# Both PSUM banks of the fourth convolution group: matmuls first, then casts

## The chip, the cores and the metric

The kernel runs on one core of one Trainium2 chip. The metric is the device time of one execution in microseconds (us). The time before is the median of 6 runs: 434.73 us, lowest 433.61, highest 435.31. The engines are written as in the profile: PE is TensorE (PEld its weight loads), ACT is ScalarE, DVE is VectorE, POOL is GpSimd, SP is SyncE. L342 is line 342 of the kernel before.

## What is computed

A light convolution over time (8 heads of 24 channels, 7 taps, causal, softmaxed taps) is followed by an RWKV channel mix. Shapes: x is 8 x 4160 x 192, the hidden width is 1024.

```python
# attn: w = softmax(weight); y[b,s,c] = sum_k w[head(c),k] * x_pad[b,s+k,c]
x_prev = np.concatenate([np.zeros((B, 1, D)), x[:, :-1, :]], axis=1)   # x is y from above
xk = mu_k * x + (1.0 - mu_k) * x_prev
xr = mu_r * x + (1.0 - mu_r) * x_prev
k = np.maximum(xk @ w_k, 0.0)
v = k * k @ w_v
r = 1.0 / (1.0 + np.exp(-(xr @ w_r)))
return (r * v).astype(np.float32)
```

## The kernel before

**The work.** The 8 sequences are taken as 4 pairs. A pair's 4160 rows are cut into steps of up to 512 rows (the first pair begins with a step of 256, and the last rows of all pairs make the last step). For each step DVE forms `d` (L472), `xk` and `xr` (L495, L499) from the transposed convolution `yT`; PE multiplies `xk` by `w_k` into `ps_k` tiles (L519); ACT takes the ReLU to `k_sb` (L548); DVE squares it to `k` (L562); PE multiplies `xr` by `w_r` (L593) and ACT takes the sigmoid (L601); PE multiplies `k` by `w_v` into `ps_v` (L576); DVE multiplies by the sigmoid into `o_sb` (L617); SP stores it.

**The order.** It is written out by hand, per engine, in bundles. A bundle has four slots, each one `ps_k` tile of 6 matmuls. Within a bundle the calls come in this order: loads due (`early`), the four K tiles and their ReLUs, `r`, transposes due (`first`), `v`, the mixes, three squares, `v_out`, the convolutions due (`xt`), the fourth square, then `late`. Each engine keeps this order for its own instructions.

**PSUM.** Every matmul result goes to one pool, `ring`: four buffers of two banks each. A new tile takes a buffer that an older tile has left, and its first matmul waits until the reader of the older tile is done.

**The convolution.** It is done in groups of blocks. The first pair's first four groups (3, 4, 4 and 5 blocks of 120 rows) are cast to `y` and transposed on PE (`tr`, L419, copied by DVE at L428 into `yT`). All later groups use 64-row pieces (`conv_mm` at L321, `conv_out` at L384), are written to DRAM (`y_write`, L400) and read back transposed (`y_read`, L406).

The change is in `conv_full`, which is called for the fourth group alone (g = 3, 5 blocks, rows 1320 to 1919 of the first pair), twice (c = 0 and c = 1), both in bundle 1. One call covers four heads. It takes one `ring` tile, two heads in each of its two banks; a bank gets two matmuls (L342, 240 columns each), and then its 48 columns per block are cast by ACT to `y` (L351). Columns are cut at multiples of 64, so that a bank takes one cast (120x480) or two (120x160 and 120x320): c = 0 has one and then two, c = 1 has two and then one. Six casts in all.

Around it, in bundle 1: the K tiles k4 to k7, `r`, the transposes of the third group (g = 2), then the two `conv_full` calls; then bundle 2: K tiles k8 to k11, `r`, the transposes of g = 3 (two tiles: four blocks, one block), `v`, two units of the fifth group's convolution; then k12 and on. The ring buffers go round accordingly: the two convolution tiles take the buffers of k6 and k7, k8 and k9 those of `r` and the transposes, k10 and k11 those of the two convolution tiles; the next `r`, the two transpose tiles and `v` take those of k8 to k11.

Of the kernel before, what the change touches and what calls it, by code (L numbers as in the profile page):

```python
# [14 lines left out]
def kernel(  # L15
# [60 lines left out]
    n = 0  # L76
# [109 lines left out]
    n = groups[0][2] * 2 * D  # L186
# [113 lines left out]
    def pieces(c0, c1):  # L300
        cuts = [c0] + [a for a in range(Q, D, Q) if c0 < a < c1] + [c1]
        return list(zip(cuts, cuts[1:]))
# [28 lines left out]
    def conv_full(g, c, copy):  # L331
        nb = groups[g][2]
        if c == 0:
            ys[g] = two.tile([P, GB, 2 * D], BF16, tag="y", name="y")
        y = ys[g][:BLK, :nb, :].rearrange("p n (c s q) -> p n c s q", c=NC, s=2)
        ps2 = ring.tile([P, 2, BANK], FP32, tag="k", name="ps_c")
        w = 2 * G
        for k in range(2):
            ps = ps2[:, k, 0 : nb * 2 * w].rearrange("p (n s c) -> p n s c", n=nb, s=2)
            for i in range(2):  # L340
                h = 4 * c + 2 * k + i
                nc.tensor.matmul(  # L342
                    out=ps[:, :, :, i * G : (i + 1) * G],
                    lhsT=toe[:, h, :],
                    rhs=xbs[g][:, :nb, :, h * G : (h + 1) * G],
                    start=True,
                    stop=True,
                )
            c0 = (4 * c + 2 * k) * G
            for a, b in pieces(c0, c0 + w):  # L350
                copy(  # L351
                    out=y[:, :, a // Q, :, a % Q : a % Q + b - a], in_=ps[:BLK, :, :, a - c0 : b - c0]
                )
# [300 lines left out]
    def conv(g, c):  # L654
        if g < 3:
            act_, dve_ = nc.scalar.copy, nc.vector.tensor_copy
            return conv_small(g, (act_, act_, dve_ if g == 0 else act_))
        if g == 3:
            return conv_full(g, c, nc.scalar.copy)
        conv_mm(g, c)  # L660
        conv_out(g, c, nc.scalar.copy)
# [153 lines left out]
```

## Time and profile before

| | |
|---|---|
| median of 6 runs | 434.73 us |
| profiled execution | 434.74 us |
| its span, first to last instruction | 433.0 us |
| mean granted TensorE clock | 0.996 |
| busy: PE, DVE, ACT, POOL | 97%, 87%, 80%, 14% of the span |
| HBM traffic over the span | 156 GB/s |
| L342, matmuls of `conv_full` | 8 of 262 to 268 ns, 23.4 to 26.5 us |
| L351, casts of `conv_full` | 6 of 292 to 700 ns, 24.1 to 26.8 us |

The profiled execution lies at the median. Some 1.7 us of its time lie outside the span. PE, DVE and ACT are all well filled, and so the averages say little about one place: the change touches 3 us near the start, and what it meets there is read from the timeline of those microseconds, engine by engine. In a timeline row the columns are start, duration of the row (neighbouring instructions of one kind are merged), engine, line, operation, output and input, count, and in brackets the idle time before it with what ended it.

### The profile page before, as it was taken

Reading aid. Unit: us, or ns where it says so; the run is one execution under the profiler, and the core shown is the slowest. Engines: PE = TensorE matmul, PEld = TensorE weight load, DVE = VectorE, ACT = ScalarE, POOL = GpSimd, SP = SyncE. Lnnn points to the kernel's source line nnn. Section 1 sums busy time; section 2 is a strip of 40 time slices with the busy share of each in tenths; the row PEclk is TensorE's granted clock in tenths of the full one; section 3 lists DMA queues with packets and bytes.
Section 4 is the critical chain, followed back from the end, with each engine's and each line's share of the span. In section 5 each row is a group of like instructions: output and inputs, shape, how many; then the busy total and the mean of one; then the engine's idle time right before and its main releaser. Section 6 shows DMA issues by size and latency. Waiting matters only on the chain.

```text
span 433.0 us, 12070 instructions
## 1 busy us (share of the span) xinstructions
PE 419.4 (97%) x5045; PEld 293.5 (68%) x5045; DVE 377.2 (87%) x678; ACT 348.0 (80%) x427; POOL 62.4 (14%) x101
## 2 busy tenths in 40 slices
PE   7779999999999999999999999999999999999995
PEld 3447677667867766776677667766766776667785
DVE  5859978888988899888889989888898889999983
ACT  5786988888988888888889878988898888777780
POOL 7661002113300200303030200203000000000000
PEclk9989999999999999999999999999999999999999
DMA  7998694999796976679796994496846484321223
GB/s 130 192 159 125 170 188 105 197 218 205 175 186 177 177 195 124 97 189 169 181 185 161 184 205 108 97 224 131 182 122 132 117 204 88 111 66 47 74 75 109
DMA packets 136444, 64.73 MB, mean 149 GB/s; under 512 B 87122, under 2 KB 136006, under 8 KB 136390
## 3 DMA queue, kind: packets, MB, share of 16 engines
q1 hardware_dynamic: 96536, 48.29, 46.7%
q0 software_dynamic: 38960, 15.08, 29.9%
q8 instruction: 39, 0.64, 0.6%
q10 hardware_dynamic: 894, 0.61, 0.5%
q14 instruction: 15, 0.12, 0.1%
HBM read 30.75 MB, written 36.96 MB: 156 GB/s over the span
## 4 chain that ended last, share of the span: by engine, by line
PE 90%; ACT 3%; DVE 3%; DMA 2%; issue 1%; POOL 1%; DVEq 0%; ACTq 0%
PE ps_v L576 40%; PE ps_k L519 38%; PE ps_r L593 7%; PE ps_c L321 4%; ACT k_sb L548 2%; DMA wk<-in_moe_w_k_dram 2%; DVE k L562 1%; DVE o_sb L617 0%; POOL xb L155 0%; ACT y L351 0%; PE ps_t L419 0%; ACT y L384 0%; DVE yT L428 0%; DVE xk L499 0%; DVE xk L495 0%
## 5 line engine op out<-in xcount | busy, mean ns | idle before, releaser
L548 ACT ACTIVATE k_sb<-ps_k 128x1024 bf16<-128x1024 f32 x260 | 246.3, 1046 | 23.1 <-PE ps_k L519 22.7
L519 PE MATMUL ps_k<-xk,wk 64*128 64x512 bf16 (+1 forms) x1632 | 182.2, 370 | 2.9 <-ACT k_sb L548 1.2
L576 PE MATMUL ps_v<-wv,k 128*128 128x192 bf16 x2080 | 182.7, 246 | 0.5 <-ACT k_sb L548 0.5
L576 PEld LDWEIGHTS <-k 128*128 128x128 bf16 x2080 | 168.6, 98 | 10.5 <-issue 10.4
L562 DVE TENSOR_TENSOR k<-k_sb 128x1024 bf16<-128x1024 bf16 x260 | 167.2, 684 | 0.4 <-ACT k_sb L548 0.4
L519 PEld LDWEIGHTS <-wk 64*128 64x128 bf16 x1632 | 75.1, 94 | 89.8 <-issue 11.7
L617 DVE TENSOR_TENSOR o_sb<-ps_v,r_sb 128x768 f32<-128x768 f32 x64 | 61.2, 956 | 35.4 <-PE ps_v L576 31.6
L384 ACT CAST y<-ps_c 128x960 bf16<-128x960 f32 (+7 forms) x81 | 50.7, 667 | 45.4 <-PE ps_c L321 45.4
L134 POOL DMA_DIRECT2D xb<-in_x_dram x56 | 40.3, 732 | 205.5 <-PE ps_k L519 158.8
L601 ACT ACTIVATE r_sb<-ps_r 128x768 bf16<-128x768 f32 x65 | 56.0, 862 | 1.3 <-PE ps_r L593 1.3
L593 PEld LDWEIGHTS <-xr 64*128 64x128 bf16 x780 | 34.1, 94 | 16.2 <-DVE xb L112 1.3
L593 PE MATMUL ps_r<-wr,xr 64*128 64x192 bf16 x780 | 42.9, 243 | 0.9 <-DVE xb L112 0.8
L499 DVE TENSOR_TENSOR xr<-xr,yT 128x1536 bf16<-128x1536 bf16 (+1 forms) x33 | 31.0, 939 | 1.1
L472 DVE TENSOR_TENSOR d<-yT 128x1536 bf16<-128x1536 bf16 (+2 forms) x35 | 31.1, 888 | 0.7 <-DMA yT<-y_dram 0.6
L499 DVE TENSOR_TENSOR xk<-xk,yT 128x1536 bf16<-128x1536 bf16 (+1 forms) x32 | 30.4, 950 | 1.1
L495 DVE TENSOR_SCALAR xk<-d,mu 128x512 bf16<-128x512 bf16 (+1 forms) x99 | 30.3, 361 | 1.2
L495 DVE TENSOR_SCALAR xr<-d,mu 128x512 bf16<-128x512 bf16 (+1 forms) x102 | 29.3, 343 | 0.0
L321 PE MATMUL ps_c<-xb,toe 64*64 64x240 bf16 (+1 forms) x448 | 20.0, 265 | 0.0
L321 PEld LDWEIGHTS <-toe 64*64 64x64 bf16 x448 | 8.3, 105 | 7.7 <-issue 7.7
L456 POOL COPY y_tail<-yT 128x195 bf16<-128x195 bf16 x4 | 1.5, 383 | 69.6 <-DMA yT<-y_dram 69.6
L428 DVE COPY yT<-ps_t 128x720 bf16<-128x720 bf16 (+1 forms) x7 | 3.2, 500 | 6.5 <-PE ps_t L419 6.5
L131 POOL DMA_DIRECT2D xb<-in_x_dram x14 | 7.6, 544 | 1.4 <-POOL xb L114 0.9
(55 smaller groups left out, 58.5 us busy)
## 6 DMA issues: line engine op xcount, KB each, us to landing
out_dram<-o_sb SPq DMA_DIRECT2D x128, 192.0 KB
xb<-in_x_dram POOLq DMA_DIRECT2D x36, 240.0 KB, 6.5
y_dram<-y SPq DMA_DIRECT2D x22, 360.0 KB
xb<-in_x_dram POOLq DMA_DIRECT2D x10, 216.0 KB, 5.2
y_dram<-y SPq DMA_DIRECT2D x22, 75.0 KB
y_dram<-y SPq DMA_DIRECT2D x6, 216.0 KB
xb<-in_x_dram POOLq DMA_DIRECT2D x6, 144.0 KB, 5.9
xb<-in_x_dram POOLq DMA_DIRECT2D x4, 192.0 KB, 7.6
```

What stands on the lines that cost most here:

```text
L134: nc.gpsimd.dma_start(out=xb[i * Q : (i + 1) * Q, full[0] : full[-1] + 1, s, :], in_=bass.AP(tensor=x.tensor, offset=x.offset + (b * S + b ...
L321: nc.tensor.matmul(out=ps[j * Q : (j + 1) * Q, i, 0 : nb * w].rearrange("p (n s c) -> p n s c", n=nn, s=2)[:, :, :, k * G : (k + 1) * G], ...
L384: copy(out=y[:, :, :, a // Q, :, a % Q : a % Q + b - a], in_=src[:, :, :, :, a - c0 : b - c0])
L495: nc.vector.tensor_scalar(out=t[:, c, :L], in0=d[:, c, :L], scalar1=mu[:, i, c : c + 1], scalar2=None, op0=ALU.mult)
L499: nc.vector.tensor_tensor(out=o, in0=o, in1=y_of(s, sl, 0), op=ALU.add)
L519: nc.tensor.matmul(out=ps[:, i, f * L : (f + 1) * L], lhsT=wk[r, c, fs], rhs=xk[r, c, :L], start=c == 0 and f == 0, stop=c == NC - 1 and f ...
L548: nc.scalar.activation(out=k_sb, in_=ps.rearrange("p a b -> p (a b)"), func=AF.Relu)
L562: nc.vector.tensor_tensor(out=o, in0=i, in1=i, op=ALU.mult)
L576: nc.tensor.matmul(out=o, lhsT=k2s[s][:, f, t * P : (t + 1) * P], rhs=wv[:, f, :], start=(f == 0), stop=(f == NF - 1),)
L593: nc.tensor.matmul(out=ps[:, i, k * D : (k + 1) * D], lhsT=xr[q, c, ts], rhs=wr[q, c, :], start=c == 0, stop=c == NC - 1,)
L601: nc.scalar.activation(out=r_sbs[s, j], in_=ps[:, :, 0 : 2 * D], func=AF.Sigmoid)
L617: nc.vector.tensor_tensor(out=o_sb.rearrange("p (b t) d -> p b (t d)", b=2), in0=v_ps.pop((s, j)), in1=r_sbs.pop((s, j)), op=ALU.mult,)
```

## The change

In `conv_full` the loop over the two banks is split in two: first the four matmuls of both banks, then the casts of both. The instructions, their operands and the order of the casts among themselves stay as they were.

```diff
-        for k in range(2):
-            ps = ps2[:, k, 0 : nb * 2 * w].rearrange("p (n s c) -> p n s c", n=nb, s=2)
+        banks = [ps2[:, k, 0 : nb * 2 * w].rearrange("p (n s c) -> p n s c", n=nb, s=2) for k in range(2)]
+        for k, ps in enumerate(banks):
             for i in range(2):
                 h = 4 * c + 2 * k + i
                 nc.tensor.matmul(
...
                     start=True,
                     stop=True,
                 )
+        for k, ps in enumerate(banks):
             c0 = (4 * c + 2 * k) * G
             for a, b in pieces(c0, c0 + w):
                 copy(
```

## The prediction

> **What bounds the kernel now.** I read the page first (who is busy), then the busy time by stages, then the timeline of PE, ACT and DVE around L342 and L351, and last the stages' clock.
>
> ```profile
> PE 419.4 (97%) x5045; PEld 293.5 (68%) x5045; DVE 377.2 (87%) x678; ACT 348.0 (80%) x427; POOL 62.4 (14%) x101
> ```
>
> ```profile
> 200.00:300.00 100.00, 100.00 (x1221) 69.68 (x1219) 90.12 (x157) 84.85 (x104) 15.52 (x26) 1.00 0.85 165
> 300.00:428.50 128.50, 128.44 (x1551) 92.88 (x1548) 113.54 (x197) 98.36 (x116) 1.28 (x3) 1.00 0.46 113
> ```
>
> In the second view the columns are the stretch, its length, busy time of PE, PEld, DVE, ACT and POOL, then the granted clock. From 61 us on PE has no idle time worth naming: whatever reaches PE earlier at 61 us ends the kernel earlier by the same amount. So the question is how much earlier PE gets through the first 61 us, where it does stand still.
>
> PE around the change:
>
> ```profile
> 22.71 0.80 PE L419 MATMUL ps_t<-ident,y_small 120*128 120x120 bf16 x12
> 23.35 0.37 PE L342 MATMUL ps_c<-xb,toe 128*128 128x240 bf16 x2
> 24.83 0.57 PE L342 MATMUL ps_c<-xb,toe 128*128 128x240 bf16 x4 [1.10 <-ACT y L351]
> 26.43 0.36 PE L342 MATMUL ps_c<-xb,toe 128*128 128x240 bf16 x2 [1.03 <-ACT y L351]
> 26.73 4.45 PE L519 MATMUL ps_k<-xk,wk 64*128 64x512 bf16 x24
> 31.01 0.66 PE L593 MATMUL ps_r<-wr,xr 64*128 64x192 bf16 x12
> ```
>
> The second bank's matmuls wait for the first bank's cast, in both calls: 1.10 and 1.03 us. The row of four is bank 1 of the first call and bank 0 of the second: the second tile's buffer was free already. The 24 matmuls after them take 4.45 us; the same 24 take 2.70 us later in the chain. The clock says why:
>
> ```profile
> 16.57:19.97 3.40, 2.06 (x21) 1.07 (x22) 3.37 (x7) 3.40 (x7) 1.97 (x4) 1.00 1.60 191
> 23.37:26.77 3.40, 1.27 (x13) 0.71 (x12) 3.18 (x7) 2.55 (x7) 2.49 (x4) 1.00 1.59 189
> 26.77:30.18 3.41, 3.41 (x19) 1.24 (x20) 2.14 (x5) 2.28 (x3) 0.89 (x2) 0.50 1.55 185
> ```
>
> After the stretch with the two waits (PE busy 1.27 of 3.40 us) the clock was 0.50 for 3.41 us; after one with 2.06 of 3.40 it stayed at 1.00.
>
> ACT, and then DVE, in the same time:
>
> ```profile
> 23.39 0.94 ACT L601 ACTIVATE r_sb<-ps_r 128x768 bf16<-128x768 f32 x1
> 24.08 0.70 ACT L351 CAST y<-ps_c 120x480 bf16<-120x480 f32 x1
> 25.23 1.15 ACT L351 CAST y<-ps_c 120x160 bf16<-120x160 f32 x4 [0.45 <-PE ps_c L342]
> 26.83 0.56 ACT L351 CAST y<-ps_c 120x480 bf16<-120x480 f32 x1 [0.45 <-PE ps_c L342]
> 28.20 1.02 ACT L548 ACTIVATE k_sb<-ps_k 128x1024 bf16<-128x1024 f32 x1 [0.82 <-PE ps_k L519]
> 29.48 3.02 ACT L548 ACTIVATE k_sb<-ps_k 128x1024 bf16<-128x1024 f32 x3 [0.26 <-PE ps_k L519]
> ```
>
> ```profile
> 26.41 2.49 DVE L562 TENSOR_TENSOR k<-k_sb 128x1024 bf16<-128x1024 bf16 x4
> 28.85 0.06 DVE L112 MEMSET xb<- 1x1 uint32 x1
> 32.45 1.22 DVE L428 COPY yT<-ps_t 128x720 bf16<-128x720 bf16 x3 [3.54 <-PE ps_t L419]
> ```
>
> ACT stands still four times for PE, and DVE 3.54 us for the transposes of the fourth group. From 32.45 to 44.19 DVE runs without a gap and PE waits for it twice (0.61 us for `xk`, 0.28 us for `o_sb`). So this stage is a relay: casts, ReLUs, transposes, DVE.
>
> **The change, step by step.** Nothing is added or removed: 8 matmuls and 6 casts before and after, no DMA and no queue passed. Moved are four matmuls, ahead of the casts that they waited for.
>
> *PE.* In the row of four, starts are about (0.57 - 0.26)/3 = 0.10 us apart. The eight run from 23.35 to about 24.35; the second tile's buffer comes free with k7's ReLU at 23.62, in time. k8 needs the buffer of `r`, whose sigmoid ends at 24.33. So k8 starts at 24.4 instead of 26.73, with 0.12 us a matmul; k10 needs the first call's casts, done at about 25.4. k11 is done by 27.3.
>
> *ACT.* The first cast now waits for all four matmuls of its tile (23.35 + 0.31 + 0.26 = 23.92), but ACT is in the sigmoid until 24.33, which hides it; with no such cover it would cost some 0.2 us. The casts then run without the two 0.45 us gaps: 24.33, 0.46 for the first, 1.16 for the next four, 0.46 for the last: done at 26.4. The four ReLUs follow at once, 0.905 us apart (the spacing of k5 to k7's, 20.68 to 23.39): ends 27.3, 28.2, 29.1, 30.0; the sigmoid ends at 30.7. Before, k11's ReLU ended at 32.50.
>
> *Transposes and `v`.* The first transpose tile needs k9's buffer (28.2): 12 transposes of 0.75 us, done 29.0. The second needs k10's (29.1), done 29.4. `v` needs k11's (30.0): 2.75 us to 32.8, the fifth group's 16 matmuls 0.55 us to 33.35. Its `xb`: the last of four loads was issued by 18.1 and took 9.1 us, so it is there at 27.2.
>
> *DVE.* Free from 28.91, it copies from 29.05 to 30.27 (1.22 us); before to 33.67: 3.4 us earlier. `xk` follows 2.78 us later, at 33.05 (36.45 before). k12 starts when PE is through, 33.4 instead of 36.51: 3.1 us earlier, its 0.61 us wait gone. The wait for `o_sb` goes too: DVE's end of it moves from 44.19 to 40.8; PE gets there at 33.4 + 7.72 - 0.28 = 40.8. That is 44.23 - 40.8 = 3.4 us for PE.
>
> *Until 61 us* PE waits twice more for a ReLU (0.25 and 0.24 us), a cycle of ACT (6.96 us a bundle) that stays. ACT's casts of bundle 3 follow PE's 3.1 us and those of bundle 4 its 3.4, so 0.1 us of the 3.4 may stay on ACT: I take **3.3 us**. The way of `y` through DRAM, on which DVE waited 0.55 us at 58.7, starts from those casts and moves with them. Against the profiled execution: 434.74 - 3.3 = **431.4 us**, which is the same against the median of 434.73.
>
> *Bounds.* The gain cannot pass DVE's idle 3.54 us by more than the two later waits, 0.5 us: 4.0 us. At the other end the two waits removed at PE with nothing of the clock would give 2.1 us, and 1.6 us if a slow stretch follows (below). Near the top, since the transposes hang on ACT's row of casts and ReLUs, which does not depend on the clock of k8 to k11.
>
> [...]
>
> **The rivals.**
>
> *The slow clock moves on.* In the new 26.8 to 30.2 PE waits for the ReLUs: busy for k11's 0.5, `r` 0.67, the transposes 0.8 and 0.3, about 2.3 of 3.4 us. That is above the 2.06 that was followed by full clock and far from 1.27; where between them the fall begins, no row shows, and in other executions the stretch may begin elsewhere. If it falls, `v` and the convolution after 30.2 run at half rate for 3.41 us and lose 1.7: a gain of 1.6, **433.1 us** (432.3 to 433.7).
>
> *Nothing comes of it.* Either the second bank's matmuls still wait for something, or a transfer with a time of its own takes the gain back: `yT` from DRAM at 58.7 is the one on which DVE waits. For it: the DMA engines are full until 30 us. Against it: the loads of the fifth group are there 5 us before use, and the stores follow the casts. **434.7 us**.
>
> *Slower.* A ring buffer goes to the tile that asks when one is free; an earlier release can change who gets which, and the change of partners can last. If a K tile got the buffer that `v` leaves late, PE would wait for `o_sb` as it does once now, 0.28 us, in each of the 57 bundles after 61 us: 16.0 - 3.3 = 12.7 us, **447.4 us**. It decides from 3.3/57 = 0.06 us a bundle. For it: that wait exists, at 43.96. Against it: the steady bundles show no such wait, and the sequence of tiles is the same.
>
> **How the numbers follow.** The forecast has 0.75 (own range 430.6 to 432.3), the slow clock 0.12, nothing 0.08, slower 0.05. The time is the forecast's, 431.4. The range 430.5 to 433.5 takes in the forecast and most of the slow clock, about 0.85. A measurement of this kernel tells 0.2% (0.87 us) from no change: faster has 0.86 (the first two cases, less a slow tail), same 0.08, slower 0.06.
>
> **What would show it.** L342's eight matmuls in one row of about 1 us from 23.35, with no wait for L351; six casts in one row, done at 26.4; 24 matmuls of k8 to k11 in about 2.9 us from 24.4; DVE's copies at L428 starting near 29.0; k12 at 33.4; granted clock 1.00 from 20 to 40 us; PE's first row after 61 us some 3.3 us earlier. Wrong it would be if L342 still waited, if the clock were 0.5 in the stretch of `v`, if k12 came less than 2 us earlier, or if PE showed a new wait after 61 us.

## The result, and the profile after

The changed kernel takes 433.43 us, the median of 40 runs, against 434.99 us for the kernel before in 82 runs on the same chips. The ratio is 0.9976, 95% interval 0.9966 to 0.9986: about 1.0 us. That is the distance of the means (435.04 and 433.99), while the medians are 1.56 us apart; the runs are of two kinds, as the first experiment shows, and the median passes from one kind to the other. The profiled execution takes 433.12 us where that of before took 434.74: 1.62 us. The prediction said 3.3 us. The sign and the place were right, the size was two to three times too large.

PE in the changed kernel (timeline; start, duration, what, idle time before it). Lines behind L348 carry a number one higher than before.

```profile
22.64 0.81 PE L420 MATMUL ps_t<-ident,y_small 120*128 120x120 bf16 x12
23.29 0.98 PE L342 MATMUL ps_c<-xb,toe 128*128 128x240 bf16 x8
24.30 2.79 PE L520 MATMUL ps_k<-xk,wk 64*128 64x512 bf16 x24
28.20 0.67 PE L594 MATMUL ps_r<-wr,xr 64*128 64x192 bf16 x12 [1.11 <-ACT k_sb L549]
29.11 1.24 PE L420 MATMUL ps_t<-ident,y 120*128 120x120 bf16 x15 [0.24 <-ACT k_sb L549]
30.95 2.80 PE L577 MATMUL ps_v<-wv,k 128*128 128x192 bf16 x32 [0.60 <-ACT k_sb L549]
33.68 0.60 PE L321 MATMUL ps_c<-xb,toe 64*64 64x240 bf16 x16
34.22 3.60 PE L520 MATMUL ps_k<-xk,wk 64*128 64x512 bf16 x24
```

The eight matmuls are one row, the 24 after them start at 24.30 and take 2.79 us: both waits and the half-rate stretch are gone. From there on PE waits for ACT three times, and the 24 matmuls of bundle 3, at 34.22, take 3.60 us with no wait named. ACT and DVE show why:

```profile
24.00 2.22 ACT L352 CAST y<-ps_c 120x480 bf16<-120x480 f32 x6
27.13 3.77 ACT L549 ACTIVATE k_sb<-ps_k 128x1024 bf16<-128x1024 f32 x4 [0.91 <-PE ps_k L520]
30.76 0.84 ACT L602 ACTIVATE r_sb<-ps_r 128x768 bf16<-128x768 f32 x1
34.13 1.88 ACT L385 CAST y<-ps_c 128x960 bf16<-128x960 f32 x3 [2.53 <-PE ps_c L321]
35.88 3.81 ACT L549 ACTIVATE k_sb<-ps_k 128x1024 bf16<-128x1024 f32 x4
```

```profile
26.35 2.49 DVE L563 TENSOR_TENSOR k<-k_sb 128x1024 bf16<-128x1024 bf16 x4
28.78 0.06 DVE L112 MEMSET xb<- 1x1 uint32 x1
29.94 1.22 DVE L429 COPY yT<-ps_t 128x720 bf16<-128x720 bf16 x3 [1.10 <-PE ps_t L420]
```

The six casts end at 26.22, as foreseen, but the first ReLU starts only at 27.13. That is 0.91 us in which ACT stood still, put down to PE, whose 24 matmuls end at 27.09. Yet k8's own six were done near 25.1. DVE's square of k4, the first of the four at 26.35, ends near 27.03, and this was the other suspect.

The clock by stretches, in the changed kernel (length, busy time of PE, PEld, DVE, ACT, POOL, then granted clock, DMA share and GB/s), and a stretch far behind:

```profile
23.37:26.77 3.40, 3.38 (x34) 1.99 (x32) 3.25 (x7) 2.84 (x8) 2.42 (x4) 1.00 1.59 189
26.77:30.18 3.41, 1.93 (x31) 1.37 (x28) 2.31 (x6) 3.05 (x4) 0.96 (x3) 1.00 1.56 189
...
200.00:300.00 100.00, 100.00 (x1222) 69.58 (x1218) 90.29 (x158) 84.85 (x104) 14.73 (x24) 1.00 0.86 167
```

PE is the bound behind 61 us as it was. So `v` tells the tale: it starts at 30.95 instead of 32.56, 1.61 us earlier, and just that reaches the end (the span is 431.4 us for 433.0). DVE's copies come 2.51 us earlier (29.94 for 32.45), of which 0.9 us does not reach PE.

### The profile page after: what moved, and what is told of

Its sections match the earlier page's. It is cut to its first block, busy times and chain, and to the rows that moved or that the text cites. A ratio compares the mean times of both kernels' runs of the same rounds, so it can differ in the third digit from the quotient of the medians.

```text
span 431.4 us, 12070 instructions
## 1 busy us (share of the span) xinstructions
PE 418.7 (97%) x5045; PEld 293.5 (68%) x5045; DVE 377.5 (87%) x678; ACT 347.7 (81%) x427; POOL 62.5 (14%) x101
## 4 chain that ended last, share of the span: by engine, by line
PE 90%; ACT 3%; DVE 2%; DMA 2%; issue 1%; POOL 1%; ACTq 0%
PE ps_v L577 41%; PE ps_k L520 37%; PE ps_r L594 7%; PE ps_c L321 4%; ACT k_sb L549 2%; DMA wk<-in_moe_w_k_dram 2%; DVE k L563 1%; PE ps_t L420 1%; ACT y L385 0%; POOL xb L155 0%; DVE yT L429 0%; DVE xk L496 0%; DVE xk L500 0%; DVE d L473 0%; PE ps_c L342 0%
## 5 line engine op out<-in xcount | busy, mean ns | idle before, releaser
L496 DVE TENSOR_SCALAR xk<-d,mu 128x512 bf16<-128x512 bf16 (+1 forms) x99 | 30.4, 363 | 1.2
L496 DVE TENSOR_SCALAR xr<-d,mu 128x512 bf16<-128x512 bf16 (+1 forms) x102 | 29.3, 342 | 0.0
L714 PE MATMUL warm<-zeros,ones_t 128*128 128x512 bf16 x16 | 6.5, 591 | 1.8 <-DVE zeros L729 1.8
```

What stands on the lines that cost most here:

```text
L496: nc.vector.tensor_scalar(out=t[:, c, :L], in0=d[:, c, :L], scalar1=mu[:, i, c : c + 1], scalar2=None, op0=ALU.mult)
```

## The experiments

Theory A is about the clock, B about the 0.91 us, C about the pace from 34 to 61 us, D about spread that showed up on the way. Unless said otherwise a diff is against the changed kernel.

### The kernel before, once more

No edit.

> The kernel before once more, for the granted clock of each of its runs. Theory A (1.2 us of the 1.62 us gained in the profiled execution are the half-rate stretch that is no longer there): runs of two kinds, some near 433.5 us with a mean granted clock of 0.999 or 1.000, most near 434.9 with 0.996, which is what one stretch of 3.41 us at half rate makes of the mean over 433 us. Rival (the two waits themselves are the gain): no such grouping, 434.7 also at a clock of 1.000. Ratio to before 1.000.

12 runs with a median of 435.14 us, ratio 1.0014 (0.9995 to 1.0033). By mean granted clock, 33 runs of the kernel before on this chip fall apart as theory A has it: 17 have 0.996 or less and take 434.6 to 436.7 us; most of the others (12 of 16) have 0.998 to 1.000 and take 433.3 to 433.9. Of the 12 runs made here, nine have 0.996 or less. A mean of 0.992, which several runs of both sets have, is more than one stretch: a loss of 0.008 of 433 us takes some 6.9 us at half rate, which is two stretches (an estimate; no kept trace shows such a run). The profiled execution happened to have no half-rate stretch (PE, then a stretch of the clock):

```profile
26.42 0.36 PE L342 MATMUL ps_c<-xb,toe 128*128 128x240 bf16 x2 [1.03 <-ACT y L351]
26.72 2.76 PE L519 MATMUL ps_k<-xk,wk 64*128 64x512 bf16 x24
...
31.41 2.80 PE L576 MATMUL ps_v<-wv,k 128*128 128x192 bf16 x32 [0.53 <-ACT k_sb L548]
```

```profile
26.77:30.18 3.41, 3.41 (x42) 1.83 (x42) 2.16 (x5) 3.15 (x4) 0.87 (x2) 1.00 1.56 185
```

With both waits in place, but at full clock, `v` starts at 31.41. So of the 1.61 us between the two profiled executions 32.56 - 31.41 = 1.15 us is the clock, and 31.41 - 30.95 = 0.46 us is the reordering itself. Counted from L342's first matmul (23.35, 23.38 and 23.29 us in the three traces) it is 1.18 and 0.37 us. This execution still took 434.67 us, since it met something else, a late transfer (PE's and DVE's waits after 60 us):

```profile
PE ps_k L519 <- DVE o_sb L617: 0.9, 1, 0.9
...
DVE d L472 <- DMA yT<-y_dram: 1.1, 1, 1.1
```

`d` at 83.9 us waited for the `yT` read that SP had issued at 70.74.

### Six k_sb buffers

```diff
-    four = ctx.enter_context(tc.tile_pool(name="four", bufs=4))
+    four = ctx.enter_context(tc.tile_pool(name="four", bufs=6))
```

> The changed kernel with six k_sb buffers in place of four. Theory B: the ReLU of k8 started at 27.13 and not at 26.2, where the casts ended, since it takes the buffer of k4, whose square ended at 27.04 on DVE. With six buffers it starts near 26.2, v near 30.1 instead of 30.95, and the execution is 0.8 us shorter than the changed kernel: 432.3 us. Rival (the ReLU waited for the end of the 24 matmuls of PE, as the profile names it): it still starts at 27.1, and the time stays at 433.1 us.

ACT, and then PE:

```profile
24.11 2.21 ACT L352 CAST y<-ps_c 120x480 bf16<-120x480 f32 x6
26.01 3.99 ACT L549 ACTIVATE k_sb<-ps_k 128x1024 bf16<-128x1024 f32 x4
```

```profile
30.05 2.80 PE L577 MATMUL ps_v<-wv,k 128*128 128x192 bf16 x32 [0.60 <-ACT k_sb L549]
32.78 0.60 PE L321 MATMUL ps_c<-xb,toe 64*64 64x240 bf16 x16
33.40 3.52 PE L520 MATMUL ps_k<-xk,wk 64*128 64x512 bf16 x24
...
40.63 2.76 PE L520 MATMUL ps_k<-xk,wk 64*128 64x512 bf16 x24
```

The ReLUs follow the casts without a gap, and everything behind is 0.9 us earlier (`v` 30.05 for 30.95, the K tiles of bundle 4 40.63 for 41.52). Theory B holds: the `k_sb` buffer was what the ReLU waited for, and the name in the profile, PE, was the wrong one. The median is 432.90 us, ratio 0.9948 (0.9928 to 0.9967). The ten runs are of two kinds, 432.2 to 432.5 and 433.3 to 433.5; the profiled one, 433.36, is of the second, with `d` 1.1 us late again. The 432.3 us that were expected are those of the first kind.

### The first wait filled with matmuls

Against the kernel before; both tiles are taken in the first call.

```diff
...
         for k in range(2):
+            if c == 0 and k == 1:
+                for _ in range(10):
+                    nc.tensor.matmul(
+                        out=conv_ps[g, 1][:, 0, 0:240], lhsT=ones_t, rhs=zeros[:, 0:240], start=True, stop=True
+                    )
```

> The kernel before, with its two waits of PE, but ten matmuls of 240 columns in the first of them, written to the second call's buffer, which is overwritten later. Theory A: the clock stays at 1.00, the 24 matmuls after the convolution take 2.8 us instead of 4.45, still from 26.7; v starts near 31.3 instead of 32.56, and the execution takes 433.5 us: three quarters of the gain of the change without its reordering. Rival (the waits are the gain): 434.7 us. [...]

```profile
23.98 1.19 PE L344 MATMUL ps_c<-zeros,ones_t 128*128 128x240 bf16 x10
25.14 0.57 PE L350 MATMUL ps_c<-xb,toe 128*128 128x240 bf16 x4
26.74 0.36 PE L350 MATMUL ps_c<-xb,toe 128*128 128x240 bf16 x2 [1.03 <-ACT y L359]
27.04 2.76 PE L527 MATMUL ps_k<-xk,wk 64*128 64x512 bf16 x24
```

For the clock the theory holds: in all 12 runs the mean clock is 0.997 or more, where 17 of 33 runs of the kernel before were at 0.996 or less. In these runs, filling 1.1 us with matmuls that compute nothing kept the stretch away. For the time the expectation failed: a median of 434.77 us, ratio 0.9992 (0.9975 to 1.0009), and only three runs at 433.4 to 434.0. In the profiled run, 435.63 us, DVE waited 1.7 us for a late `yT`, and PE 0.7 us for a late `xb` load and 0.6 us for `o_sb`, all between 80 and 95 us. Why this kernel meets late transfers more often is open.

### The convolution ahead of v, with six buffers

The six buffers are as above.

```diff
+            if 2 <= b <= 5:
+                run(xt, b)
             run(vq, b)
...
-            run(xt, b)
+            if not 2 <= b <= 5:
+                run(xt, b)
```

> The changed kernel with six k_sb buffers and, in bundles 2 to 5, the fifth and sixth groups' convolution ahead of v. Theory C: from 34 to 61 us ACT sets the pace (7.31, then 6.96 us from one bundle's casts to the next), because its casts wait behind v; an advance of DVE there is worth nothing. With the casts ahead of v, k13 to k15 no longer wait for ACT in bundle 3, and the 0.24 us waits of PE for a ReLU go in bundles 4 and 5: 0.7 to 1.2 us less than with six buffers alone, 431.3 us. Rival (DVE sets the pace there): the time is that of the six buffers alone, 432.3 us.

This failed: 434.27 us, ratio 0.9983 (0.9964 to 1.0002), slower than with the six buffers alone. The K tiles of bundle 3 did run in 2.76 us, as theory C says, but now `v` waits for a ReLU (0.52 us in bundles 3 to 5) and ACT for the K tiles behind `v`:

```profile
42.20 3.77 ACT L549 ACTIVATE k_sb<-ps_k 128x1024 bf16<-128x1024 f32 x4 [1.17 <-PE ps_k L520]
45.83 0.84 ACT L602 ACTIVATE r_sb<-ps_r 128x768 bf16<-128x768 f32 x1
46.52 1.93 ACT L385 CAST y<-ps_c 128x960 bf16<-128x960 f32 x3
49.62 3.77 ACT L549 ACTIVATE k_sb<-ps_k 128x1024 bf16<-128x1024 f32 x4 [1.17 <-PE ps_k L520]
```

From one bundle to the next takes 7.42 us instead of 6.96. The reading that fits is that PE and ACT go round in a ring over four PSUM buffers, where this order only moves the gap to another place and widens it by 0.46 us; that is argued from this trace and not varied further.

### DVE made late

```diff
...
             run(vq, b)
+            if b == 2:
+                for _ in range(2):
+                    nc.vector.tensor_tensor(out=idle_t, in0=zeros, in1=zeros, op=ALU.add)
             run(mixes, b)
```

> The changed kernel with two additions of 128x512 on DVE (about 0.35 us each) ahead of d in bundle 2; their result is not used. Theory C (the ReLUs and casts on ACT set the pace from 34 to 61 us, and DVE has room): k12 starts 0.7 us later, but the K tiles of bundle 4 start where they did (41.5 us), 0.2 us later at most. Rival (DVE sets the pace there, as the prediction had it): they start 0.7 us later, at 42.2 us.

```profile
34.88 2.76 PE L521 MATMUL ps_k<-xk,wk 64*128 64x512 bf16 x24 [0.79 <-DVE xk L501]
...
41.43 0.82 PE L521 MATMUL ps_k<-xk,wk 64*128 64x512 bf16 x6
42.61 2.12 PE L521 MATMUL ps_k<-xk,wk 64*128 64x512 bf16 x18 [0.35 <-DVE o_sb L619]
```

Counted from the start of `v` in bundle 2 (30.76 here, 30.95 in the changed kernel's profile), the K tiles of bundle 4 start 10.67 us later, 10.57 without the delay; `v` of bundle 4 starts 14.40 us later, 14.27 without. So DVE comes 0.8 us later and PE loses 0.1 (one execution). The row of bundle 3 takes 2.76 us now and not 3.60: started later, its tiles find their buffers free. The time is 433.03 us. From 34 us on PE and ACT set the pace, and a delay of 0.8 us on DVE is nearly all absorbed.

### The changed kernel, two more traces

> The changed kernel once more, for its trace. Its 41 runs were of two kinds: 24 at 432.9 to 433.7 us, 17 at 434.0 to 437.2, of these 12 with a mean clock of 0.991 to 0.996. Theory A: in a run of the second kind a half-rate stretch follows the waits of PE for ReLUs between 27 and 31 us, or yT arrives about 1 us late near 83 us. In a run of the first kind neither is seen.

432.96 us, no half-rate stretch. It bears out theory B without an edit, for here the wait is put down to DVE's square:

```profile
26.65 3.77 ACT L549 ACTIVATE k_sb<-ps_k 128x1024 bf16<-128x1024 f32 x4 [0.82 <-DVE k L563]
```

The expectation that a run of the quick kind shows no late `yT` did not hold: here `d` waited 0.7 us for it, and PE lost 0.2 us by that.

> The changed kernel a third time, for its trace: as for the second.

434.98 us, mean clock 0.996 (of the 41 runs whose clock is listed, 11 have 0.996 or less, not 12 as written above). Two stretches, and then PE:

```profile
27.33:30.74 3.41, 1.78 (x27) 1.41 (x27) 2.31 (x6) 3.41 (x4) 1.53 (x3) 1.00 1.41 167
30.74:34.15 3.41, 3.21 (x21) 3.03 (x21) 3.34 (x8) 0.85 (x2) 2.97 (x5) 0.50 1.06 114
```

```profile
30.94 4.33 PE L577 MATMUL ps_v<-wv,k 128*128 128x192 bf16 x32 [0.60 <-ACT k_sb L549]
35.20 0.60 PE L321 MATMUL ps_c<-xb,toe 64*64 64x240 bf16 x16
35.73 3.60 PE L520 MATMUL ps_k<-xk,wk 64*128 64x512 bf16 x24
```

The half rate has moved behind the new waits for ReLUs: `v` takes 4.33 us for 2.80, and the bundle after it starts 1.51 us later (35.73 for 34.22). `d` waited for `yT` here too, 0.5 us. This is the prediction's first rival, in about a quarter of the runs by their mean clock.

### Six buffers, and yT read one bundle earlier

```diff
-    four = ctx.enter_context(tc.tile_pool(name="four", bufs=4))
+    four = ctx.enter_context(tc.tile_pool(name="four", bufs=6))
...
-            at(late, xs[-1] + (1 if g == 4 else 2), y_read, g)
+            at(late, xs[-1] + 1, y_read, g)
```

> The changed kernel with six k_sb buffers, and each yT read from DRAM issued one bundle (6.3 us) earlier for the groups after the fifth. Theory D: the runs with six buffers were of two kinds, five at 432.2 to 432.5 us and five at 433.3 to 433.5, and the second kind is the one whose yT arrives 1.1 us late near 83 us (as in the profiled run). With the earlier read all runs lie near 432.3 us, and DVE waits for no yT after 60 us. Rival (the two kinds have another cause, or the earlier read holds up the stores queued behind it on SP): two kinds as before, or slower.

All eight runs take 431.85 to 432.47 us, ratio 0.9955 (0.9940 to 0.9971). With six buffers alone SP issued the read at 69.38 and `d` had to wait; now SP issues it at 63.41 and `d` does not (DVE in the two kernels):

```profile
82.56 0.96 DVE L473 TENSOR_TENSOR d<-yT 128x1536 bf16<-128x1536 bf16 x1 [1.10 <-DMA yT<-y_dram]
```

```profile
81.01 0.96 DVE L473 TENSOR_TENSOR d<-yT 128x1536 bf16<-128x1536 bf16 x1
```

Theory D holds in these eight runs. This version is quicker than both kernels: its slowest run is below the quickest of the changed kernel (432.90 us).

### The same two edits, with the old and the new order on one chip

> The kernel before, its matmuls and casts in the old order, with six k_sb buffers and the yT reads one bundle earlier. Theory: in the old order the ReLU of k8 waits for PE, not for a buffer, and the two waits of PE stay, so the six buffers bring nothing; the earlier read only takes the late yT away. Half-rate runs (mean clock 0.996 and less) stay as frequent as before: a median of 434.0 to 434.7 us, the quickest runs at 433.3 to 433.6. Rival (the buffers and the read are the gain, not the order): near 432.2 us, as with the new order.

> The changed kernel with six k_sb buffers and the yT reads one bundle earlier, a second time, on one chip with the old order: 431.9 to 432.5 us in all runs, no mean clock under 0.997. Rival (the first time was a good chip): runs above 433 us.

Old order: 433.66 us, ratio 0.9985 (0.9967 to 1.0003); seven runs at 433.4 to 433.7, and five of 12 with a mean clock of 0.996 or less, at 434.6 to 435.7. That is somewhat better than expected, with fewer half-rate runs (10 of 17 in the kernel before on this chip; too few to tell apart). New order: 432.18 us, ratio 0.9936 (0.9914 to 0.9958), no mean clock under 0.997; five runs at 432.0 to 432.3 and one, against expectation, at 433.42. In runs at full clock the new order is worth 433.5 - 432.2 = 1.3 us once the ReLUs can follow. With four buffers it is 433.61 - 433.26 = 0.35 us, between the medians of the runs with a clock of 0.997 or more that take less than 434 us (12 of the kernel before on one chip, 24 of the changed kernel).

## Why the prediction was too large

*The stage at the change: right.* One row of eight matmuls, k8 at 24.4 (24.30), the 24 matmuls at full clock in 2.9 us (2.79), casts done at 26.4 (26.22), the first cast's longer wait hidden by the sigmoid. PE in the profiled execution has no wait after 61 us.

*"The four ReLUs follow at once": this step failed, 0.9 us.* The prediction counted what a ReLU reads and the PSUM buffer it frees, but not the buffer it writes. `k_sb` has four, and k8's is that of k4, whose square on DVE runs from 26.35 to 27.03. With six buffers the steps behind it came out as they had been worked out: DVE's copies at 29.05 (predicted 29.05), `v` at 30.05 (30.05), k12 at 33.40 (33.4).

*The step from DVE to PE: failed, 0.8 us.* The prediction took PE's later gain from DVE's lead, 3.4 us at the `o_sb` of bundle 3. With six buffers DVE's lead there was 43.23 - 40.20 = 3.0 us (its three products for `xk`, L496, took 1.17 us, 0.88 before; why is open), and PE did not get that much either: `v` of bundle 4 came only 46.83 - 44.32 = 2.5 us earlier, the lead that `v` of bundle 2 had (32.56 - 30.05). Its casts hold ACT, the ReLU of k12 comes behind them, and k13 to k15 wait for the buffers of both: in the changed kernel the tiles of the row that takes 3.60 us start at 34.22, 35.14, 36.06 and 36.99, where the casts of the two convolution tiles end at 35.09 and 36.01 and k12's ReLU at 36.94. The prediction had seen that cycle of ACT (6.96 us a bundle) and allowed 0.1 us for it; what arrived is `v`'s lead, and nothing of DVE's beyond it. The late DVE run, 0.8 us on DVE for 0.1 on PE, shows it from the other side. So the 3.3 us are, within 0.1, the 1.6 that came, 0.9 of the buffers and 0.8 of the step from DVE to PE.

*The ground it was measured from: incomplete.* 1.15 of the 1.61 us in the traces are the half-rate stretch, and this is not in every run of the kernel before: 17 of 33, and 9 of the 12 behind them. One trace looked like the median and was one kind of run. What the change does to the median is to make such runs rarer (11 of 41), and to shorten the rest by 0.35 us. The mean over all runs weighs both kinds and moves by 1.05 us; the two traces are one of each kind and differ by 1.62.

*The rivals.* The slow clock was priced at a loss of 1.7 us behind `v` and measured at 1.5; it was given 0.12 and comes in about a quarter of the runs. The same slip probably helped it: with ReLUs 0.9 us later PE was busy 1.93 us (26.77 to 30.18 in the profiled execution) and 1.78 us (27.33 to 30.74 in the third trace) of 3.41, not 2.3, and with six buffers (2.33 busy) none of the 24 runs with both six buffers and the convolution behind `v` had a mean clock under 0.997. The transfer with a time of its own exists, the `yT` read, but in both kernels, and it takes 1 us in some runs rather than the whole gain. The lasting change of buffers was not seen.

*The gaps ahead of the half rate.* In the first trace of the kernel before half rate followed on gaps of 1.10 and 1.03 us, and with ten matmuls in the first of them (the filled wait) the mean clock was 0.997 or more in all 12 runs. In the profiled execution of the changed kernel no slow stretch stayed at 26.8 to 30.2: the clock there is 1.00.

## What to carry to other kernels

When an engine is to start earlier, list every buffer that the instruction needs, the one it writes too, and who leaves it last; here 0.9 us of the gain stopped at the four buffers of `k_sb`, and two more let it through. Follow a lead around the whole ring of engines: here the smaller lead, that of `v`, arrived, and not that of DVE, which had been waiting longest. And before a sum is made against one trace, look whether the runs fall into kinds by the granted clock: here the part of the gain that lay in the clock was a change of odds (a mean clock of 0.996 or less in 43 of 75 runs before, in 11 of 41 after), not a fixed time.

## What the runs showed of the hardware

The half-rate stretches lasted 3.41 us each time (26.8 to 30.2 us in the first trace of the kernel before, 30.7 to 34.1 in the third of the changed kernel). They followed on 3.4 us stretches with PE busy for 1.27 us (23.37 to 26.77) and 1.78 us (27.33 to 30.74), and not, in the same executions, on 2.06 (16.57 to 19.97 in the first) and 2.58 (20.51 to 23.92 in the second). The length of a gap does not tell the two apart in the first trace: the longest one near the change, 1.21 us ahead of 18.52, lies in the stretch with 2.06 us, and the full clock followed.

The kernel before had the same waits in two traces, and the half rate in one: in the second PE was busy for 1.29 us from 23.37 to 26.77, and the clock stayed at 1.00. The same was seen with the old order and both edits (1.29 us too). So PE's busy time in such a stretch does not by itself say whether the half rate follows; what else does was not shown. In the first trace the clock falls at 26.79, is full again at 30.21 and falls a last time, behind PE's last matmul, at 432.98; from 30.21 to there it is 118.0 times the 3.413 us of the half-rate stretch. In the second it is 1.00 from 16.57 to 428 us wherever it was read, and 0.80 from 428 to 434 us.

43 of the 75 runs of the kernel before whose clock is listed had a mean clock of 0.996 or less, and 11 of 41 of the changed kernel.

The `yT` read near 70 us was there no later than 12.0 us after its issue in the two profiled executions of before and after (issued at 71.89 and 70.28, used without a wait at 83.91 and 82.29). In others it took longer: 13.2 us in the second trace of the kernel before and with six buffers, and 13.8 with the filled wait, where DVE waited 1.1, 1.1 and 1.7 us for it. What makes it late is open.
